# Regrouped early routing, marks shared between two engines, a contiguous overflow list and smaller expert capacities in an attention-plus-experts kernel

## Chip, cores and metric

The kernel runs on one core of a Trainium2 chip. The metric is the device time of one execution in microseconds (us). Three runs of the kernel before gave 647.88, 653.0 and 653.28 us; their median is 653.0 us. One further execution was profiled.

The engines are named as in the profile: PE multiplies matrices (PEld is its weight load), DVE is the vector engine, ACT the scalar engine, POOL the general-purpose engine, SP the engine from which most DMAs are issued. An engine executes its own instructions in order.

## What is computed

Linear attention without a softmax, a normalization of each head, and then a mixture of eight experts in which each token goes to the one expert with the largest logit.

```
kv = einsum('bhsd,bhse->bhde', k, v)            # 8 batches, 8 heads, 576 tokens, 64 columns
out = einsum('bhsd,bhde->bhse', q, kv)
x = out / sqrt(mean(out*out, -1) + 1e-6) * g_norm   # x: 4608 tokens x 512
logits = x @ w_gate;  e_idx = argmax(logits)
gate_w = softmax(logits)[e_idx];  eom = sigmoid(x @ w_output_gate)
for e in range(8):
    mask = e_idx == e
    y[mask] = gate_w[mask] * eom[mask, e] * (relu(x[mask] @ w1[e]) @ w2[e])   # 512 -> 1024 -> 512
```

## The kernel before

**Tiles.** The 4608 tokens are 36 tiles of 128 rows. Attention of a batch is `kv_part` (L413, the product of k and v in five pieces), `kvT_part` (L443, two transposes) and `m_part` (L452); `out_tile` (L482) then makes one tile of 128 tokens, and ACT copies it, squares it and copies its gate products (L512 to L515). The squares are summed by DVE (L528). Tiles are routed in groups: `GR = (8, 8, 10, 10)`. `route` (L532) is a generator of small DVE steps for one group: the norm, the logits, the choice of the expert as a one-hot `ohb` (L607), then on PE a count of earlier tokens of the same expert `rps` (L635 to L644), the token's slot `slots`, and for each tile a mark `la` (L686), a 128x128 matrix that is 1 where the slot's place within its tile is the column. PE multiplies the marks with the slot's tile number, `tblps` (L714), into a table of which token stands in which place; the table gives the row numbers `gidx` for gathers and `oidx` for the scatter of results. `advance` (L748) takes every group that is being routed one step further, up to its next `yield 1`. `PLACES` (L66) says which engine makes the marks of a group: P is POOL, V is DVE.

**Runs.** The experts run in 16 runs (`RUNS`, L54). The first eight take 256 rows of each expert out of the first 16 token tiles (`EARLY = 16`); the last eight take the rest of each expert, in order of how many rows it has, so many rows as `CAP` (L38) leaves for that rank: 704, 704, 640, 620, 600, 576, 576, 576 less 256. Rows beyond the capacity would go through a loop after the last run (L1045), one tile of 128 rows at a time, that loads the expert's weights anew. `mm1` (L272) is the first product of a run, 8 times 12 matmuls whose moving side has as many columns as the run has rows; `mm2` (L295) is the second, for each tile of 128 rows 24 matmuls of 512 columns. Where a run ends in a tile of exactly 64 rows, `half` (L268) is 64 and that tile takes 16 matmuls (L311): the high and the low part of the first product stand side by side. Weights are loaded raw (`wload`, L183, one DMA of 512 KB from SP) and each is split into a high and a low part (`split`, L192, ACT and DVE).

**Order.** Order is written by hand inside the `manual_schedule` blocks. `early` (L769) does the first four batches (`FIRST_B`), tiles 0 to 15, and the routing of the groups 0 and 1; during `while routing` (L803) PE gets eight matmuls on a constant (`constant`, L408, `COLD[2]`) for each round of `advance`. Then come the loads of the second weights of run 0 and the first gather. `late` (L811) is the generator of all other attention and routing; `run` (L971) takes one piece of it after each of its 8 `mm1` steps and one within each `mm2` of the first runs. Loads of the early part go to 22 buffers (`free`), those of the late part to 8 (`xfree`), all issued by SP in order; the writes of x to memory, `xs`, are on SP too. The gathers (`gather`, L228) and the scatters of results (L328) are indirect DMAs from POOL, and POOL also scales gathered rows (`scale_rows`, L243).

**The overflow list.** While runs 7 and 8 go, `overflow_list` (L905) makes a list of the tiles beyond the capacities: `met`, 128 partitions by 44 entries by 2 values. SP writes one of the two values of each entry to memory:

```
959    met = sm.tile([P, NOVER, 2], F32, name="met")
969    nc.sync.dma_start(out=tab, in_=met[:, :, 0])
```

Of the kernel before, what the change touches and what calls it, by code (L numbers as in the profile page):

```python
# [11 lines left out]
F32 = mybir.dt.float32  # L12
# [22 lines left out]
C_SCALE = DM + H  # L35


CAP = [704, 704, 640, 620, 600, 576, 576, 576]  # L38


EARLY = 16
TA = 2
ROWS_A = TA * P
CMAX = max(CAP) - ROWS_A
TMAX = 6

NOVER = NT + E

GR = (8, 8, 10, 10)
GROUPS = [list(range(sum(GR[:i]), sum(GR[:i+1]))) for i in range(len(GR))]  # L50
GMAX = max(GR)
EARLY_GROUP = [sum(GR[:i + 1]) for i in range(len(GR))].index(EARLY)
# [10 lines left out]

APART = (1, 2, 3)

PLACES = ['P', 'PV', 'P', 'P']  # L66

COLD = (2, 20, 8)

ROUND = 1.5 * 2.0 ** 30  # L70

# [51 lines left out]
def body(ctx: ExitStack, tc: tile.TileContext, kvm, rem, qT, wg, gn, w1, w2, kc, xs, tab, out):  # L123
# [143 lines left out]

    def half(i):  # L268

        return P // 2 if RUNS[i][2] % P == P // 2 else 0  # L270

    def mm1(i, f):  # L272

        C = RUNS[i][2]
        T = half(i)
        hi, lo = ([a[:, d] for d in range(4)] for a in xT[i])
        wh, wl = wgt[(1, f // 2)]
        if f == 0:
            w = i // E
            hT[i] = rp_[w].tile([P, 8, 2 * (ROWS_A, CMAX)[w]], F32R, name="hT", tag="hT")  # L280
        ps = ps_h.tile([P, 512], F32, name="hps", tag="h")
        for d in range(4):
            o = d * 256 + (f % 2) * P
            for w, x, k in ((wh, hi, 0), (wh, lo, 1), (wl, hi, 2)):
                nc.tensor.matmul(ps[:, :C], w[:, o:o + P], x[d][:, :C],  # L285
                                 start=(d == 0 and k == 0), stop=(d == 3 and k == 2))
        h = hT[i][:, f]
        nc.scalar.activation(h[:, 0:C], ps[:, :C], AF.Relu)  # L288
        for a, b, l in [(0, C - T, C + T)] + ([(C - T, C, C)] if T else []):
# [5 lines left out]
    def mm2(i, k, events):  # L295
        nonlocal ny
        t, c0, M = tiles_of(i)[k]
        C = RUNS[i][2]
        T = half(i)
        ps = ps_y[0].tile([P, DM], F32, name="yps", tag=f"y{ny % 2}")  # L300
        tl = tails.pop((i, t))
        for f in range(8):
            h = hT[i][:, f]
            wh, wl = wgt[(2, f // 2)]
            w0 = (f % 2) * DM
            w = [a[:, w0:w0 + DM] for a in (wh, wl)]
            if M == T:

                for b in (1, 0) if f == 0 else (0, 1):
                    rows = M + b * M  # L310
                    nc.tensor.matmul(ps[:rows], h[:, c0:c0 + rows], w[1 - b],  # L311
                                     start=(f == 0 and b == 1), stop=(f == 7 and b == 1))
            else:
                hh, hl = h[:, c0:c0 + M], h[:, C + T + c0:C + T + c0 + M]
                for n, (a, b) in enumerate(((hh, w[0]), (hh, w[1]), (hl, w[0]))):
                    nc.tensor.matmul(ps[:M], a, b, start=(f == 0 and n == 0), stop=(f == 7 and n == 2))  # L316
            for e in events.get(f, ()):
                e()
        y = mem.tile([P, DM], F32, name="y", tag=f"y{ny % 3}")
        ny += 1  # L320
        if M == T:
            y2 = mem.tile([P, DM], F32, name="y2", tag="yb")
            nc.scalar.copy(y2[:M], ps[M:2 * M])
# [50 lines left out]
    nq = 0  # L374
    for b in range(B):
        loads += [(kvt, (b, c), kvm[b][:, c]) for c in range(4)]
        if b == 0:
            loads.append((rt, 0, rem[0][0:P // 2]))
        elif b % 2 == 0:
            loads.append((rt, b // 2, rem[b // 2]))  # L380
        if b == 1:
            loads.append((rt, 0, rem[0][P // 2:]))

        bq = b - 1 if b == 0 else b
        while bq >= 0 and nq < -(-tiles_ready(bq) * P // QC):
            loads.append((qt, nq, qT[nq]))
            nq += 1
        if b == B - 1:
            while nq < NTOK // QC:
                loads.append((qt, nq, qT[nq]))  # L390
                nq += 1

    late_loads = [l for l in loads if (l[1] >= EARLY // 2 if l[0] is qt else 2 * l[1] >= FIRST_B if l[0] is rt else l[1][0] >= FIRST_B)]
    loads = [l for l in loads if not any(l is x for x in late_loads)]

    def load(loads, free, spare=0):

        while loads and len(free) > spare:
            where, k, src = loads.pop(0)
            n = src.shape[0]  # L400
            if k in where:
                nc.sync.dma_start(out=where[k][P - n:], in_=src)
                continue
            t = take([P] + list(src.shape[1:]), F32, "ld", free)
            nc.sync.dma_start(out=t[:n], in_=src)
            where[k] = t

    def constant(ps, n, start):  # L408
# [4 lines left out]
    def kv_part(b):  # L413
# [3 lines left out]
        for s in range(5):  # L417
# [17 lines left out]
                give(kvt.pop((b, s)))  # L435
            elif b % 2:
                give(rt.pop(b // 2))
        nc.scalar.copy(augs[b % 3][:, :, 0:D], ps[:, 0:NP * D].rearrange("q (p d) -> q p d", p=NP))
        cp = wk.tile([P, NP * D], F32, name="kvc", bufs=1)
        nc.vector.tensor_copy(cp, ps[:, 0:NP * D])  # L440
        yield cp

    def kvT_part(cp):  # L443
# [88 lines left out]
    def route(gi):  # L532
# [176 lines left out]
        vec.tensor_tensor(out=xtail[:, g0:g0 + n, C_SCALE - DM], in0=se[:, :n], in1=eo[:, :n], op=ALU.mult)  # L709
        xwrite(g0, xs[1 + g0 * P:1 + (g0 + n) * P, DM:XW].rearrange("(t p) x -> p t x", p=P), xtail[:, g0:g0 + n])  # L710
        yield from pause(8)
        tps = ps_t.tile([P, 2, E * TMAX], F32, name="tblps", tag="t")
        for t in range(n):
            nc.tensor.matmul(tps, las[t], rc[:, t, 0:2], start=(t == 0), stop=(t == n - 1))  # L714
# [54 lines left out]
    def early():  # L769

        def more():
            load(loads, free)
            if not loads and not opened[0]:
                open_rows()
            while not loads and w1s and free:
                wload(0, 1, w1s.pop(0))

        w1s = list(range(4))

        more()  # L780
        for b in range(FIRST_B):
            lim = min(tiles_ready(b - 1) if b else 0, EARLY)
            kv = kv_part(b)
            next(kv)
            more()
            run_out(lim)
            next(kv)
            cp = next(kv)
            more()
            run_out(lim)  # L790
            kvT = kvT_part(cp)
            run_out(lim)
            run_out(lim)
            m_part(b, kvT)
            more()
            while run_out(lim):
                more()
        while run_out(EARLY):
            more()
        while squares:  # L800
            sums()
        load(late_loads, xfree, 2)
        while routing:  # L803
            advance()
# [100 lines left out]
    def overflow_list():  # L905
# [63 lines left out]
        nc.sync.dma_start(out=tab, in_=met[:, :, 0])

    def run(i, unit):  # L971

# [170 lines left out]
```

## Time and profile before

| what | us |
|---|---|
| median of three runs | 653.0 |
| the profiled execution, its own time | 652.84 |
| its span, first to last instruction | 651.0 |
| attention, tiles 0 to 15 and routing of groups 0 and 1 | 0 to 83.0 |
| first gather to first expert matmul | 83.0 to 96.2 |
| runs 0 to 6, with the late attention between them | 96.2 to 317.1 |
| run 7 | 317.1 to 346.5 |
| run 8 | 346.5 to 404.9 |
| run 9, of the same size as run 8 | 404.9 to 445.8 |
| runs 10 to 15, to the last matmul | 445.8 to 637.9 |

The span is the profiled execution from its first to its last instruction; 1.84 us of its time lie around it. A row of the timeline gives the start, the duration (or the time to the end of the last, where several are merged), the engine, the line, and in brackets how long the engine had been idle and what ended that. A row of the windows gives a stretch of the span, the busy time of PE, PEld, DVE, ACT and POOL in it with their instructions, the clock that PE was granted as a share of full speed, the share of the 16 DMA engines and the GB/s.

### The profile page before, as it was taken

How to read it: one execution, taken by the hardware profiler on the slowest of the kernel's cores; microseconds unless marked ns; L12 is line 12 of the kernel's file. 1: busy time of each engine (PE TensorE's matmuls, PEld its weight loads, DVE VectorE, ACT ScalarE, POOL GpSimd, SP SyncE). 2: the span in 40 equal slices, each digit the busy share in tenths (PEclk: the TensorE clock that was granted, in tenths of full speed). 3: DMA queues.
4: the chain of work that ended last, by engine and by line, in shares of the span. 5: the costliest groups of instructions: out<-in, count | busy, mean ns of one | idle time of the engine just before them, and what ended most of it. 6: DMA issues, size and time to landing. Idle time of an engine off the chain costs nothing.

```text
span 651.0 us, 12185 instructions
## 1 busy us (share of the span) xinstructions
PE 575.8 (88%) x4825; PEld 498.1 (77%) x4825; DVE 338.1 (52%) x644; ACT 285.7 (44%) x481; POOL 169.6 (26%) x163
## 2 busy tenths in 40 slices
PE   6776829999998988899989759999999999999991
PEld 5664619888887876789878647989899888988881
DVE  1128525645476888575685314544626363647430
ACT  1355015565656844256454213443536353535420
POOL 1001330030303271703613013315050505151101
PEclk9678768999999999899989978999999999999996
DMA  8996465779895573665929977426364645464200
GB/s 287 376 401 243 144 257 180 296 264 360 311 327 205 195 256 120 182 208 179 292 86 122 19 114 252 172 97 210 116 204 143 204 142 190 153 204 135 70 17 17
DMA packets 48395, 126.21 MB, mean 194 GB/s; under 512 B 15490, under 2 KB 15618, under 8 KB 48336
## 3 DMA queue, kind: packets, MB, share of 16 engines
q1 hardware_dynamic: 41440, 105.19, 51.8%
q0 software_dynamic: 6464, 20.00, 10.4%
q8 instruction: 39, 0.64, 0.4%
q10 hardware_dynamic: 432, 0.22, 0.1%
q14 instruction: 20, 0.16, 0.1%
HBM read 106.19 MB, written 19.99 MB: 194 GB/s over the span
## 4 chain that ended last, share of the span: by engine, by line
PE 59%; issue 10%; DMA 8%; DVE 7%; POOL 4%; ACT 2%; POOLq 0%; SPq 0%; DVEq 0%; ACTq 0%
PE yps L316 26%; PE hps L285 24%; DMA wraw<-w 7%; PE tps L261 3%; POOL la L686 2%; DMA xg<-xs,gidx 2%; DVE wlo L218 2%; PE kvps L432 2%; PE ops L507 2%; PE yps L311 1%; ACT whi L215 1%; POOL out L328 1%; PE cps L411 1%; DVE ss L528 1%; DVE gp L577 1%
## 5 line engine op out<-in xcount | busy, mean ns | idle before, releaser
L285 PE MATMUL hps<-xT,whi 128*128 128x256 f32 (+5 forms) x1024 | 228.1, 314 | 10.2 <-DVE hT L290 9.3
L316 PE MATMUL yps<-whi,hT 128*128 128x512 f32 (+2 forms) x592 | 202.8, 406 | 0.0
L285 PEld LDWEIGHTS hps<-xT,whi 128*128 128x128 f32 x1024 | 172.9, 193 | 18.5 <-DVE hT L290 11.0
L285 PE MATMUL hps<-xT,wlo 128*128 128x256 f32 (+5 forms) x512 | 158.6, 310 | 0.0
L316 PEld LDWEIGHTS yps<-whi,hT 128*128 128x128 f32 (+2 forms) x592 | 112.7, 190 | 25.1
L328 POOL DMA_INDIRECT out<-y,oidx x42 | 46.2, 1100 | 299.6 <-ACT y L327 230.2
L290 DVE SCALAR_TENSOR_TENSOR hT<-hps,hT 128x256 fp32r<-128x256 f32 (+4 forms) x168 | 63.9, 400 | 109.3 <-ACT hT L288 102.1
L211 DVE SCALAR_TENSOR_TENSOR wlo<-wraw,gcol,whi 128x1024 fp32r<-128x1024 f32 x64 | 81.8, 1282 | 71.3 <-ACT whi L208 69.2
L316 PE MATMUL yps<-wlo,hT 128*128 128x512 f32 (+2 forms) x296 | 117.6, 397 | 0.0
L288 ACT ACTIVATE hT<-hps 128x256 fp32r<-128x256 f32 (+5 forms) x128 | 55.9, 437 | 140.4 <-PE hps L285 136.1
L285 PEld LDWEIGHTS hps<-xT,wlo 128*128 128x128 f32 x512 | 98.8, 193 | 0.9
L218 DVE TENSOR_TENSOR wlo<-wraw,whi 128x1024 fp32r<-128x1024 f32 x64 | 83.4, 1303 | 23.8 <-ACT whi L215 22.6
L208 ACT ACTIVATE whi<-wraw,gcol 128x1024 fp32r<-128x1024 f32 x64 | 73.3, 1150 | 20.9 <-DMA wraw<-w 20.9
L215 ACT CAST whi<-wraw 128x1024 fp32r<-128x1024 f32 x64 | 66.5, 1040 | 0.0
L241 POOL TENSOR_TENSOR xg<-xg 128x512 f32<-128x512 f32 (+3 forms) x40 | 49.0, 1226 | 67.4 <-DMA xg<-xs,gidx 66.7
L316 PEld LDWEIGHTS yps<-wlo,hT 128*128 128x128 f32 (+2 forms) x296 | 56.5, 191 | 10.5
L264 ACT CAST xT<-tps 128x512 fp32r<-128x512 f32 (+3 forms) x42 | 23.3, 557 | 64.3 <-PE tps L261 63.5
L233 POOL DMA_INDIRECT xg<-xs,gidx x42 | 47.3, 1126 | 15.8 <-issue 14.6
L327 ACT ACTIVATE y<-yps,tl 128x512 f32<-128x512 f32 (+2 forms) x37 | 25.5, 688 | 57.9 <-PE yps L316 42.4
L261 PE MATMUL tps<-ident,xg 128*128 128x128 f32 (+3 forms) x168 | 26.3, 282 | 25.1 <-DVE tl L257 15.9
L261 PEld LDWEIGHTS tps<-ident,xg 128*128 128x128 f32 (+3 forms) x168 | 20.6, 147 | 33.2 <-DVE xg L241 10.0
L686 POOL TENSOR_SCALAR la<-ni,rlon 128x128 bf16<-128x128 f32 x32 | 23.9, 763 | 83.2 <-DVE rlon L659 72.7
(146 smaller groups left out, 438.3 us busy)
## 6 DMA issues: line engine op xcount, KB each, us to landing
wraw<-w SPq DMA_DIRECT2D x128, 512.0 KB, 3.8
ld<-kvm SPq DMA_DIRECT2D x32, 512.0 KB, 7.4
ld<-qT SPq DMA_DIRECT2D x18, 512.0 KB, 5.0
xs<-xrow SPq DMA_DIRECT2D x18, 512.0 KB, 4.3
ld<-rem SPq DMA_DIRECT2D x3, 512.0 KB
xg<-xs,gidx POOLq DMA_INDIRECT x42
out<-y,oidx POOLq DMA_INDIRECT x42
ld<-rem SPq DMA_DIRECT2D x2, 256.0 KB, 10.7
```

What stands on the lines that cost most here:

```text
L208: he.activation(hi, r, AF.Copy, scale=gcol[:, 0:1])
L211: eng.scalar_tensor_tensor(out=lo, in0=r, scalar=gcol[:, 0:1], in1=hi.bitcast(F32), op0=ALU.mult, op1=ALU.subtract)
L215: he.copy(hi, r)
L218: eng.tensor_tensor(out=lo, in0=r, in1=hi.bitcast(F32), op=ALU.subtract)
L233: nc.gpsimd.indirect_dma_start(out=x[:M, :], out_offset=None, in_=rows, in_offset=bass.IndirectOffsetOnAxis(ap=gidx[i // E][:M, p, t:t + 1 ...
L241: eng.tensor_tensor(out=v, in0=v, in1=f, op=ALU.mult)
L261: nc.tensor.transpose(ps[:, c, :M], x[:M, c * P:(c + 1) * P], ident[:M, :M])
L285: nc.tensor.matmul(ps[:, :C], w[:, o:o + P], x[d][:, :C], start=(d == 0 and k == 0), stop=(d == 3 and k == 2))
L288: nc.scalar.activation(h[:, 0:C], ps[:, :C], AF.Relu)
L290: nc.vector.scalar_tensor_tensor(out=h[:, l:l + b - a], in0=ps[:, a:b], scalar=0.0, in1=h[:, a:b].bitcast(F32), op0=ALU.max, op1=ALU.subtract)
L316: nc.tensor.matmul(ps[:M], a, b, start=(f == 0 and n == 0), stop=(f == 7 and n == 2))
L328: i_ = nc.gpsimd.indirect_dma_start(out=out, out_offset=bass.IndirectOffsetOnAxis(ap=oidx[i // E][:M, RUNS[i][0], t:t + 1], axis=0), in_=y ...
```

## The change

The diff has these parts.

1. `CAP` becomes 692, 652, 632, 608, 592, 576, 570, 556, so the last eight runs have 436, 396, 376, 352, 336, 320, 314 and 300 rows, 4878 rows with the first eight in place of 4996. `half` now holds for any last tile of up to 64 rows; the high and low parts stand 64 columns apart, and columns between them are set to zero (two `memset` on DVE a run where they exist). The number of tiles of each run, and which of them are half tiles, stay as they were.
2. Groups of 10, 6, 10, 10 tiles; marks by POOL and DVE in turn in groups 0, 2 and 3, and by DVE, DVE, POOL in group 1; two more pauses ahead of `tblps` in groups 2 and 3.
3. Constants come four at a time, on a buffer of another pool, also three times a batch and once after the fourth in `early`; in `while routing`, seven rounds also take a piece of `late`: the k-v product of batch 4 in three pieces, tiles 16 and 17, the transposes and `m_part` of batch 4. The four loads of k and v of batch 4 are moved ahead of the first weights, into the 22 buffers.
4. The remainder rows of batches 0 and 1 come in one load in place of two halves. In `kv_part` DVE's copy for the transposes stands ahead of ACT's copy.
5. The second weights of run 0 are loaded behind the first gather, with a wait on a POOL instruction that stands after it.
6. `met` becomes two tiles, so that what SP writes is contiguous in each partition.
7. `early` and the runs 0 to 6 stand in one `manual_schedule` block.

```
-CAP = [704, 704, 640, 620, 600, 576, 576, 576]
+CAP = [692, 652, 632, 608, 592, 576, 570, 556]
-GR = (8, 8, 10, 10)
+GR = (10, 6, 10, 10)
-PLACES = ['P', 'PV', 'P', 'P']
-COLD = (2, 20, 8)
+PLACES = ['PV', 'VVP', 'PV', 'PV']
+COLD = (2, 20, 4)
+PIECES = 7
...
-        return P // 2 if RUNS[i][2] % P == P // 2 else 0
+        n = RUNS[i][2] % P
+        return n if n <= P // 2 else 0
...
+        C0 = C - T
+        if T % (P // 2) and f == 0:
+            for c in (C0, C0 + P // 2):
+                nc.vector.memset(hT[i].bitcast(F32)[:, :, c + T:c + P // 2], 0.0)
...
+    late_loads.sort(key=lambda l: l[0] is not kvt or l[1][0] > FIRST_B)
+    loads += late_loads[:4]
+    late_loads = late_loads[4:]
...
-        nc.scalar.copy(augs[b % 3][:, :, 0:D], ps[:, 0:NP * D].rearrange("q (p d) -> q p d", p=NP))
         cp = wk.tile([P, NP * D], F32, name="kvc", bufs=1)
         nc.vector.tensor_copy(cp, ps[:, 0:NP * D])
+        nc.scalar.copy(augs[b % 3][:, :, 0:D], ps[:, 0:NP * D].rearrange("q (p d) -> q p d", p=NP))
...
         yield from pause(8)
+        if g0 >= EARLY:
+            yield 1
+            yield 1
         tps = ps_t.tile([P, 2, E * TMAX], F32, name="tblps", tag="t")
...
+            constants(1)
             kvT = kvT_part(cp)
+            constants(1)
             run_out(lim)
             run_out(lim)
+            constants(1)
             m_part(b, kvT)
...
         while routing:
             advance()
             if routing:
-                constant(ps_t.tile([P, 512], F32, name="cps", tag="t"), COLD[2], True)
+                constants(1)
+                if n < PIECES:
+                    next(rest)
+                    n += 1
+        gather(0)
+        mark = c1.tile([P, 1], F32, name="mark")
+        behind = nc.gpsimd.memset(mark, 0.0)
         for c in range(4):
-            wload(0, 2, c)
-        gather(0)
+            d = wload(0, 2, c)
+            tc.add_manual_dep(d.ins, behind.ins.name, ...)
+
+    def constants(n):
+        constant(ps_h.tile([P, 512], F32, name="cps", tag="h"), n * COLD[2], True)
...
-        met = sm.tile([P, NOVER, 2], F32, name="met")
+        met = [sm.tile([P, NOVER], F32, name=f"met{i}") for i in range(2)]
...
-        nc.sync.dma_start(out=tab, in_=met[:, :, 0])
+        nc.sync.dma_start(out=tab, in_=met[0])
```

More of the change, by code (lines that the diff above doesn't have):

```diff
@@ L43 @@
 ROWS_A = TA * P
-CMAX = max(CAP) - ROWS_A
+CMAX = -(-(max(CAP) - ROWS_A) // (P // 2)) * (P // 2)
 TMAX = 6
 NOVER = NT + E
-GR = (8, 8, 10, 10)
+GR = (10, 6, 10, 10)
 GROUPS = [list(range(sum(GR[:i]), sum(GR[:i+1]))) for i in range(len(GR))]
@@ L287, in mm1 @@
         h = hT[i][:, f]
+        C0 = C - T
+        if T % (P // 2) and f == 0:
+            for c in (C0, C0 + P // 2):
+                nc.vector.memset(hT[i].bitcast(F32)[:, :, c + T:c + P // 2], 0.0)
         nc.scalar.activation(h[:, 0:C], ps[:, :C], AF.Relu)
-        for a, b, l in [(0, C - T, C + T)] + ([(C - T, C, C)] if T else []):
+        for a, b, l in [(0, C0, C0 + P if T else C)] + ([(C0, C, C0 + P // 2)] if T else []):
             nc.vector.scalar_tensor_tensor(out=h[:, l:l + b - a], in0=ps[:, a:b], scalar=0.0,
@@ L309, in mm2 @@
                 for b in (1, 0) if f == 0 else (0, 1):
-                    rows = M + b * M
+                    rows = (1 + b) * P // 2
                     nc.tensor.matmul(ps[:rows], h[:, c0:c0 + rows], w[1 - b],
@@ L313, in mm2 @@
             else:
-                hh, hl = h[:, c0:c0 + M], h[:, C + T + c0:C + T + c0 + M]
+                l0 = C - T + P if T else C
+                hh, hl = h[:, c0:c0 + M], h[:, l0 + c0:l0 + c0 + M]
                 for n, (a, b) in enumerate(((hh, w[0]), (hh, w[1]), (hl, w[0]))):
@@ L322, in mm2 @@
             y2 = mem.tile([P, DM], F32, name="y2", tag="yb")
-            nc.scalar.copy(y2[:M], ps[M:2 * M])
+            nc.scalar.copy(y2[:M], ps[P // 2:P // 2 + M])
             nc.vector.tensor_tensor(out=y[:M], in0=ps[:M], in1=y2[:M], op=ALU.add)
@@ L376, in body @@
         loads += [(kvt, (b, c), kvm[b][:, c]) for c in range(4)]
-        if b == 0:
-            loads.append((rt, 0, rem[0][0:P // 2]))
-        elif b % 2 == 0:
+        if b % 2 == 0:
             loads.append((rt, b // 2, rem[b // 2]))
-        if b == 1:
-            loads.append((rt, 0, rem[0][P // 2:]))
         bq = b - 1 if b == 0 else b
@@ L399, in load @@
             where, k, src = loads.pop(0)
[L400 to L403, printed above, removed]
             t = take([P] + list(src.shape[1:]), F32, "ld", free)
-            nc.sync.dma_start(out=t[:n], in_=src)
+            nc.sync.dma_start(out=t, in_=src)
             where[k] = t
@@ L802, in early @@
         load(late_loads, xfree, 2)
+        n = 0
         while routing:
@@ L805, in early @@
             if routing:
-                constant(ps_t.tile([P, 512], F32, name="cps", tag="t"), COLD[2], True)
-        for c in range(4):
-            wload(0, 2, c)
-        gather(0)
+                constants(1)
+                if n < PIECES:
[4 more added lines that the diff above has]
+        behind = nc.gpsimd.memset(mark, 0.0)
+        for c in range(4):
+            d = wload(0, 2, c)
+            tc.add_manual_dep(d.ins, behind.ins.name,
+                              mybir.DependencyInfo(mybir.DependencyClass.Sync, mybir.DependencyReason.DATA),
+                              reason="order of the transfers")
+    def constants(n):
+        constant(ps_h.tile([P, 512], F32, name="cps", tag="h"), n * COLD[2], True)
     def late():
@@ L958, in overflow_list @@
         yield
-        met = sm.tile([P, NOVER, 2], F32, name="met")
+        met = [sm.tile([P, NOVER], F32, name=f"met{i}") for i in range(2)]
         vec.tensor_tensor(out=sel2, in0=sel, in1=c0.unsqueeze(1).to_broadcast(shp), op=ALU.mult)
-        vec.tensor_reduce(out=met[:, :, 0], in_=sel2, axis=AX.X, op=ALU.add)
+        vec.tensor_reduce(out=met[0], in_=sel2, axis=AX.X, op=ALU.add)
         yield
-        vec.tensor_tensor(out=met[:, :, 0], in0=met[:, :, 0], in1=iv, op=ALU.add)
-        vec.tensor_scalar(out=met[:, :, 0], in0=met[:, :, 0], scalar1=float(P), scalar2=None, op0=ALU.mult)
+        vec.tensor_tensor(out=met[0], in0=met[0], in1=iv, op=ALU.add)
+        vec.tensor_scalar(out=met[0], in0=met[0], scalar1=float(P), scalar2=None, op0=ALU.mult)
         vec.tensor_tensor(out=sel2, in0=sel, in1=cf[:, K_E:K_E + E].unsqueeze(1).to_broadcast(shp), op=ALU.mult)
         yield
-        vec.tensor_reduce(out=met[:, :, 1], in_=sel2, axis=AX.X, op=ALU.add)
-        vec.tensor_copy(meti, met[:, :, 1])
-        nc.sync.dma_start(out=tab, in_=met[:, :, 0])
+        vec.tensor_reduce(out=met[1], in_=sel2, axis=AX.X, op=ALU.add)
+        vec.tensor_copy(meti, met[1])
+        nc.sync.dma_start(out=tab, in_=met[0])
     def run(i, unit):
@@ L1013, in run @@
             drop(2, c)
+    rest = late()
     with tc.manual_schedule(engines=MAN):
@@ L1019, in body @@
             ps_p.clear()
-    rest = late()
-    ps_y[0] = main.enter_context(tc.tile_pool(name="ps_y", bufs=1, space=psum))
-    with tc.manual_schedule(engines=MAN):
+        ps_y[0] = main.enter_context(tc.tile_pool(name="ps_y", bufs=1, space=psum))
         split(0, 1, 0)
```

## The prediction, made before the result was known

> **What bounds the kernel now.** I read the page first (busy shares and slices), then windows cut at the stages, then the timeline where a window's PE is not full, then the chain for the price of one step.
>
> ```profile
> PE 575.8 (88%) x4825; PEld 498.1 (77%) x4825; DVE 338.1 (52%) x644; ACT 285.7 (44%) x481; POOL 169.6 (26%) x163
> PEclk9678768999999999899989978999999999999996
> GB/s 287 376 401 243 144 257 180 296 264 360 311 327 205 195 256 120 182 208 179 292 86 122 19 114 252 172 97 210 116 204 143 204 142 190 153 204 135 70 17 17
> ```
>
> PE is the bound at 88%, so what counts is where it is not busy or not at full clock. The slices, 16.3 us each, show two such places: the first six, with a clock of 6 to 8 tenths, and the 22nd to 25th, where the DMA falls to 19 GB/s and the clock then to 7.
>
> ```profile
> 61.50:83.00 21.50, 14.09 (x97) 10.50 (x95) 13.23 (x62) 0.47 (x2) 8.92 (x13) 0.76 0.55 171
> 83.00:96.20 13.20, 2.20 (x9) 1.43 (x9) 2.75 (x6) 1.23 (x3) 6.41 (x6) 0.57 0.75 297
> 96.20:131.00 34.80, 34.62 (x406) 30.03 (x407) 20.13 (x26) 20.10 (x34) 1.03 (x1) 0.92 0.66 230
> 232.40:269.00 36.60, 29.16 (x204) 24.84 (x203) 27.93 (x60) 14.88 (x24) 17.35 (x19) 1.00 0.60 188
> 346.50:404.90 58.40, 47.18 (x204) 39.41 (x203) 18.63 (x35) 16.96 (x25) 11.04 (x11) 0.88 0.94 113
> 404.90:445.80 40.90, 40.90 (x197) 35.27 (x196) 19.45 (x32) 16.67 (x23) 11.49 (x11) 1.00 0.43 142
> ```
>
> From 61.5 to 83.0 PE's work is mostly constants, and to 96.2 it waits for the gather. Run 0 (third row) leaves PE no gap. In 232.4 to 269.0 PE lacks 7.4 us. Runs 8 and 9 (last two rows) have the same 448 rows; run 8 takes 58.40 us and run 9 40.90.
>
> **The overflow list (part 6).**
>
> ```profile
> 344.52 0.66 SPq L969 DMA_DIRECT2D tab<-met  x1
> ...
> 387.79 1.15 ACT L208 ACTIVATE whi<-wraw,gcol 128x1024 fp32r<-128x1024 f32 x1 [19.96 <-DMA wraw<-w]
> ...
> DMA packets 7633, 7.10 MB, mean 118 GB/s; under 512 B 5920, under 2 KB 5920, under 8 KB 7630
> tab<-met SPq DMA_DIRECT2D x1, 22.0 KB
> ```
>
> SP sends 22 KB at 344.52. One value of each pair is taken, so it goes as 128 x 44 = 5632 pieces of 4 bytes, and the packets of 340 to 400 us (third row) hold 5920 under 512 B. The weights queued behind it reach ACT only at 387.79, after ACT sat idle for 19.96 us. A contiguous list is one piece of 176 B in each partition, 128 in all, a 44th of the count. By the two windows the jam costs 58.40 - 40.90 = 17.5 us; PE's idle time in run 8 alone is 58.40 - 47.18 = 11.2, the rest is the lower clock (0.88) and the bunching of waits. I take 17.5, since run 9 has the same matmuls, and keep 11.2 as the low end. Late next: nothing within some 40 us, as run 9 shows.
>
> **The capacities (part 1).**
>
> ```profile
> 404.85 19.46 PE hps L285 x96
> ...
> 547.77 14.08 PE hps L285 x96
> ```
>
> 448 rows take 19.46 us for the first product, 320 rows 14.08: 0.0420 us a row. The list falls by 118 rows, so 118 x 0.0420 = 5.0 us. The second product keeps its matmuls, as tiles and half tiles stay. The new zeroing on DVE waits for what `hT`'s first write waits for anyway and lies under the 12 matmuls of the first step: nothing; uncovered, eight of them at some 0.3 us (estimate from the marks' 0.326 below) would be 2.4.
>
> **The seven pieces (part 3).**
>
> ```profile
> 99.64 1.91 PE kvps L432 x32
> ...
> 103.34 0.71 PE ops L507 x32
> ...
> 105.67 1.08 PE kvps L432 x32
> ...
> 108.38 0.71 PE ops L507 x32
> ...
> 110.72 0.61 PE kvps L432 x16
> ```
>
> These are, in the chain of run 0, the pieces that move into the wait for routing. PE was full there, so 1.91 + 0.71 + 1.08 + 0.71 + 0.61 = 5.0 us leave the path (transposes and the small product left out). In their new place PE had constants. Their loads: batch 4's k and v move ahead of the first weights, on a queue that moves 287 to 401 GB/s through the first three slices; what then comes later (weights, writes of x) is needed after 80 us. The load for tiles 16 and 17 goes out after tile 15, as before. SP is moved past nothing that the routing needs, but PE is (a rival below).
>
> **Marks and pauses in group 3 (part 2).**
>
> ```profile
> 260.92 7.39 POOL L686 TENSOR_SCALAR la<-ni,rlon 128x128 bf16<-128x128 f32 x10 [2.09 <-DVE rhk L660]
> ...
> 263.53 0.30 PE L714 MATMUL tblps<-rrc,la 128*128 128x96 bf16 x3
> ...
> 268.37 0.22 PE L714 MATMUL tblps<-rrc,la 128*128 128x96 bf16 x1 [0.36 <-POOL la L686]
> ```
>
> POOL makes ten marks in 7.39 us, and PE stands behind them from 263.53 to 268.59, 5.1 us, where ten matmuls at 0.1 need 1.0. With five marks on POOL (3.7 us) and two pieces more before `tblps`, the 4.1 us go. For that DVE gets ten marks more in groups 2 and 3, at 0.326 us each (row below) 3.3 us; DVE is idle for 36.60 - 27.93 = 8.7 us in that window, yet in order, so some delay evictions that PE waits for. I charge 1.0, with 0 and 3.3 as ends. Net 3.1.
>
> **The early routing and the first gather (parts 2, 3, 5).**
>
> ```profile
> 68.50:75.20 6.70, 6.64 (x34) 5.14 (x33) 3.61 (x14) 0.47 (x2) 0.00 (x0) 0.55 0.40 130
> ...
> 70.57 0.23 DVE L607 TENSOR_TENSOR ohb<-rsc,rsx 128x64 bf16<-128x64 f32 x1
> ...
> 75.19 0.21 PE L635 MATMUL rps<-erow,row 128*128 128x72 bf16 x1
> ...
> 76.69 2.96 POOL L686 TENSOR_SCALAR la<-ni,rlon 128x128 bf16<-128x128 f32 x4 [8.38 <-PE cps L411]
> ...
> L686 DVE TENSOR_SCALAR la<-ni,rlon x4: 274/326/379, 77.0 to 78.9; 128x128 bf16<-128x128 f32 x4
> ...
> 79.38 0.17 DVE L709 TENSOR_TENSOR xtail<-rdn 128x8 f32<-128x8 f32 x1
> 80.05 1.96 SPq L188 DMA_DIRECT2D wraw<-w  x4
> ...
> 82.97 1.09 POOL L233 DMA_INDIRECT xg<-xs,gidx  x1 [3.32 <-issue]
> ...
> 89.91 0.69 DVE L241 TENSOR_TENSOR xg<-xg 128x512 f32<-128x512 f32 x1 [8.94 <-DMA xg<-xs,gidx]
> ...
> 269.83 1.00 POOL L233 DMA_INDIRECT xg<-xs,gidx  x1 [0.30 <-issue]
> ...
> 273.33 1.05 POOL L241 TENSOR_TENSOR xg<-xg 128x512 f32<-128x512 f32 x1 [1.24 <-DMA xg<-xs,gidx]
> ```
>
> The first gather starts at 82.97 and its rows are used at 89.91, 6.9 us later; four weight loads had been issued at 80.05, just ahead of it. A gather with little beside it, at 269.83, needed 3.5 us to 273.33. The second weights now wait until it has been issued, so I take 6.9 - 3.5 = 3.4 us; ends 0 (the loads follow at once and share the DMA engines) and 3.4. They then land some 4 us later, and run 0 needs them only after its first steps.
>
> The gather cannot start before the last `xtail` (79.38) is in memory. Up to there DVE bounds the routing, with two waits on PE; in one of them `ohb` is ready at 70.80 and `rps` starts at 75.19, 4.4 us behind constants. Afterwards: DVE's 13.2 us in the first window grow by 2.9 (group 0 has ten tiles and two rounds more left after tile 15, five of its marks are DVE's), plus 0.4 for batch 4's copy, less 0.8 for six tiles in place of eight: 15.7. PE between tile 15 and the second `rps` has constants, two k-v pieces, two tiles and two small products, 12 us at the low clock by the rows above doubled, so `rps` is about 1.3 late, and two groups in step save about 1.5 by overlap. 61.5 + 15.7 + 1.3 - 1.5 = 77.0, an estimate, against 79.55: 2.5 us. Ends 0 (the pieces hold the routing as the constants did) and 6 (it becomes as short as DVE's old 13.2).
>
> A page speaks against marks on both engines at once: the Trainium skill, GPSIMD Engine Reference, section 1 (SBUF interfaces), says that POOL shares its interfaces with VectorE, with contention against DVE instructions that have two SBUF inputs or run in a 2-port mode. Taken as no overlap at all, group 1's two POOL and four DVE marks would cost about 1.3 us more, and the sum would be 617.6. The trace does not show it for marks: four beside a working DVE took 2.96, ten took 7.39, 0.74 each both times. Without these sentences the sum stands as it is.
>
> The rest of parts 3, 4 and 7 I cost at nothing: constants stand where PE waits for copies (cover gone: 13 calls of four at 0.21, the low-clock price in the 6.70 us window, 11 us of PE, most of it in the first 50 us, which the loads pace); the whole remainder load brings 256 KB ahead of batch 1 and takes them away behind it; one copy ahead of the other saves at most 0.4 a batch.
>
> **Sum.** 651.0 - 17.5 - 5.0 - 5.0 - 3.1 - 3.4 - 2.5 = 614.5 us span, and with the 1.84 us around it (652.84 - 651.0) 616.3. The profiled execution stands 0.2 below the median of 653.0, so 616 holds for both.
>
> **Rivals.** (a) The pieces hold the routing. PE is in order, and a late q for tile 16 would stop everything behind it, `rps` and `tblps` too. For it: constants did just that (70.80 to 75.19). Against: the DMA share there is 0.55. Then the 2.5 are lost and as much again: 621. (b) The jam is not the list's, but that of whatever run 8 loads, or the contiguous list is still slow: 616.3 + 17.5 = 634. Against it: run 9's loads are of the same kind and stall nothing. (c) The other side: the smaller capacities overflow. The loop after the last run then makes each extra tile alone: 36 marks at 0.326 (11.7), a gather (6.9), 4 MB of weights at about 400 GB/s (10.5), its matmuls and the rest (about 9): 38 us, an estimate. One tile gives 654, no change; from two tiles on it is slower, 692. The reference's routing of its default inputs, padded to 256 early rows, gives by rank 660, 646, 620, 607, 584, 557, 556, 502 rows: all fit, one by a single row, so it is unlikely. (d) Run 8 gets back only its idle 11.2 us: 622.6, within the range.
>
> **Numbers.** My forecast, 0.78: 616, with (d) in it. (a) 0.13: 621. (b) 0.05: 634. (c) 0.04: 654 or 692, half each. The range leaves out (b) and (c) and little more: low 606 (routing 6 in place of 2.5, no charge on DVE, PE's remaining gaps in 232 to 269 closing by 4 more, and a warmer start), high 630 (early gain 0, list 11.2, DVE's charge 3.3). Faster by over 1% (about what a measurement of this kernel tells from no change) 0.96, within 1% 0.02, slower 0.02.
>
> **What would show it.** In the changed kernel's trace: run 8 about as long per row as run 9, no idle ACT before its weights; `tblps` of group 3 without gaps; no attention of batch 4 after the first expert matmul; that matmul near 90 us, the first rows used some 3.5 us after the first gather; the runs 8 to 15 shorter by 0.042 us a row. Wrong would be: run 8 still over 50 us, a first expert matmul after 95 us, new DVE waits in runs 4 to 6, or any instruction of the overflow loop.

## The result, and the profile after

The changed kernel takes 614.03 us (median of four runs, 613.19 to 614.87), the kernel before 651.46 (four runs beside them, 647.88 to 653.28). The ratio is 0.943, with a 95% interval of 0.938 to 0.948. The forecast was 616.0. The profiled execution took 614.2 us, its span 612.4.

First the page of the changed kernel: busy time of PE, then PE's clock and the DMA rate in 40 slices of 15.3 us.

```profile
PE 556.8 (91%) x4829; PEld 484.0 (79%) x4829; DVE 338.2 (55%) x666; ACT 285.7 (47%) x481; POOL 156.8 (26%) x149
PEclk9989859999999988999999999999999999999996
GB/s 310 406 405 329 328 235 220 371 256 311 234 244 200 246 155 161 241 210 202 276 157 238 129 103 209 121 162 165 151 185 125 218 145 207 141 217 137 42 19 17
```

Both weak places have shrunk. Ahead of the last slice the clock falls below 8 in one, the sixth (the first gather), and no slice ahead of the last three moves less than 103 GB/s, where one of before moved 19. PE's busy time fell by 19.0 us (575.8 to 556.8), the span by 38.6: about half the gain is idle time.

The windows of the changed kernel at the stages that the prediction showed (columns as there):

```profile
61.50:79.40 17.90, 11.86 (x193) 8.88 (x190) 14.64 (x68) 5.12 (x14) 4.82 (x7) 0.79 0.84 278
79.40:89.40 10.00, 2.79 (x9) 1.72 (x9) 2.80 (x6) 1.94 (x3) 4.61 (x6) 0.50 0.76 257
89.40:123.60 34.20, 34.19 (x411) 29.84 (x412) 21.25 (x28) 20.42 (x37) 3.36 (x3) 0.94 0.86 303
224.20:253.80 29.60, 26.69 (x181) 24.13 (x180) 22.44 (x53) 14.05 (x23) 10.51 (x11) 0.94 0.55 171
329.50:370.50 41.00, 41.00 (x202) 35.54 (x201) 18.55 (x34) 16.88 (x24) 11.38 (x11) 1.00 0.47 157
370.50:409.20 38.70, 38.70 (x197) 34.50 (x196) 19.04 (x34) 16.30 (x23) 11.36 (x11) 1.00 0.47 152
```

Run 8 (fifth row) has no idle PE and full clock; its 41.00 us for 436 rows and run 9's 38.70 for 396 are 0.094 and 0.098 us a row. Taking the first matmul of each run from the timeline, the span divides like this:

| stage | before | after | difference | predicted |
|---|---|---|---|---|
| to the first expert matmul | 96.2 | 88.7 | -7.5 | -5.9 |
| runs 0 to 3 | 136.1 | 135.4 | -0.7 | with the next row |
| runs 4 and 5 | 60.9 | 53.5 | -7.3 | -8.1 for both rows |
| run 6 | 23.8 | 23.8 | 0.0 | 0 |
| run 7 | 29.7 | 27.9 | -1.8 | 0 |
| run 8 | 58.0 | 41.0 | -17.0 | -18.0 |
| runs 9 to 15, to the last matmul | 233.2 | 229.0 | -4.2 | -4.5 |
| behind the last matmul | 13.1 | 13.1 | 0.0 | 0 |

The timeline of the changed kernel around the first gather and around the last group's marks:

```profile
64.89 0.78 PE L513 MATMUL ops<-aug,ld 64*64 64x80 f32 x32 [2.15 <-DMA ld<-qT]
...
76.34 0.17 DVE L715 TENSOR_TENSOR xtail<-rdn 128x6 f32<-128x6 f32 x1
...
79.42 1.09 POOL L236 DMA_INDIRECT xg<-xs,gidx  x1 [3.94 <-DVE wlo L214]
...
83.01 0.69 DVE L244 TENSOR_TENSOR xg<-xg 128x512 f32<-128x512 f32 x1 [4.20 <-DMA xg<-xs,gidx]
...
88.68 1.30 PE L289 MATMUL hps<-xT,whi 128*128 128x256 f32 x2 [0.68 <-ACT xT L267]
...
231.41 3.48 POOL L692 TENSOR_SCALAR la<-ni,rlon 128x128 bf16<-128x128 f32 x5 [2.59 <-DVE rlon L665]
231.43 0.50 DVE L692 TENSOR_SCALAR la<-ni,rlon 128x128 bf16<-128x128 f32 x2
...
233.46 0.70 DVE L692 TENSOR_SCALAR la<-ni,rlon 128x128 bf16<-128x128 f32 x3
234.60 0.41 DVE L299 SCALAR_TENSOR_TENSOR hT<-hps,hT 128x256 fp32r<-128x256 f32 x1
235.06 0.50 PE L289 MATMUL hps<-xT,whi 128*128 128x256 f32 x2 [2.91 <-DVE hT L299]
236.62 1.02 PE L724 MATMUL tblps<-rrc,la 128*128 128x96 bf16 x10
```

The gather starts at 79.42 (82.97 before) and its rows are used 3.6 us later (6.9 before). The late q of tile 16, the mechanism of rival (a), holds PE for 2.15 us. The ten `tblps` now go without a gap in 1.02 us, but the five marks on DVE stand in front of an `hT`, and PE waits 2.91 us for it: the charge that the prediction put at 1.0.

The chain of waits shows the price of a row as before:

```profile
329.46 18.99 PE hps L289 x96
370.47 17.28 PE hps L289 x96
...
510.00 14.07 PE hps L289 x96
```

(18.99 - 14.07) / (436 - 320) = 0.0424 us a row.

### The profile page after: what moved, and what is told of

Read it like the earlier page. It is cut to its first block, busy times and chain, and to the rows that moved or that the text cites. A ratio compares the mean times of both kernels' runs of the same rounds, so it can differ in the third digit from the quotient of the medians.

```text
span 612.4 us, 12185 instructions
## 1 busy us (share of the span) xinstructions
PE 556.8 (91%) x4829; PEld 484.0 (79%) x4829; DVE 338.2 (55%) x666; ACT 285.7 (47%) x481; POOL 156.8 (26%) x149
## 4 chain that ended last, share of the span: by engine, by line
PE 70%; issue 11%; DVE 6%; DMA 6%; ACT 3%; POOL 2%; another core or an unknown queue 1%; ACTq 0%; POOLq 0%; SPq 0%; DVEq 0%
PE yps L326 30%; PE hps L289 27%; PE ops L513 4%; PE tps L264 3%; PE kvps L438 3%; DMA ld<-qT 2%; DVE wlo L221 2%; DMA xg<-xs,gidx 1%; PE yps L320 1%; DMA wgs<-wg 1%; POOL out L338 1%; PE cps L417 1%; ACT whi L218 1%; DVE hT L299 1%; DMA xs<-xrow 1%
## 5 line engine op out<-in xcount | busy, mean ns | idle before, releaser
L289 PE MATMUL hps<-xT,whi 128*128 128x256 f32 (+8 forms) x1024 | 222.4, 309 | 10.1 <-DVE hT L299 8.8
L326 PE MATMUL yps<-whi,hT 128*128 128x512 f32 (+3 forms) x592 | 200.3, 402 | 0.0
L289 PE MATMUL hps<-xT,wlo 128*128 128x256 f32 (+8 forms) x512 | 156.2, 305 | 0.0
L326 PEld LDWEIGHTS yps<-whi,hT 128*128 128x128 f32 (+3 forms) x592 | 110.8, 187 | 24.7
L299 DVE SCALAR_TENSOR_TENSOR hT<-hps,hT 128x256 fp32r<-128x256 f32 (+9 forms) x168 | 62.9, 395 | 102.8 <-ACT hT L297 94.9
L326 PE MATMUL yps<-wlo,hT 128*128 128x512 f32 (+3 forms) x296 | 116.5, 394 | 0.0
L297 ACT ACTIVATE hT<-hps 128x256 fp32r<-128x256 f32 (+8 forms) x128 | 55.4, 433 | 118.7 <-PE hps L289 113.5
L326 PEld LDWEIGHTS yps<-wlo,hT 128*128 128x128 f32 (+3 forms) x296 | 55.6, 188 | 10.7
L244 POOL TENSOR_TENSOR xg<-xg 128x512 f32<-128x512 f32 (+8 forms) x40 | 49.4, 1240 | 33.8 <-DMA xg<-xs,gidx 32.8
L513 PE MATMUL ops<-aug,ld 64*64 64x80 f32 x1152 | 29.5, 238 | 11.1 <-DMA ld<-qT 5.1
```

Source lines behind the costliest of these rows:

```text
L244: eng.tensor_tensor(out=v, in0=v, in1=f, op=ALU.mult)
L289: nc.tensor.matmul(ps[:, :C], w[:, o:o + P], x[d][:, :C], start=(d == 0 and k == 0), stop=(d == 3 and k == 2))
L513: nc.tensor.matmul(ps[c0:c0 + D, u, p * W:(p + 1) * W], qt[g // 2][r, p, q0:q0 + D], augs[b % 3][r, p, :], start=True, stop=True)
```

## The experiments

Runs e1 to e4, e5 to e8 and e9 to e12 were each timed beside the kernel before (medians 651.24, 651.83 and 649.6). Each undoes or changes one part of the changed kernel (e10 builds on e8, e12 on e11), except e9, which starts from the kernel before. "Cost" is the median less 614.03. The intervals of the ratios are about 0.007 wide to each side, so costs of 1 or 2 us are read from the traces, not from the medians.

There is one trace of each, and the stages vary between traces too. In the changed kernel and in e1, e2, e5 and e6, which all have its early part, the last `xtail` comes between 75.7 and 77.5 us and the first expert matmul between 87.9 and 89.8. From that matmul to run 6 the changed kernel and the runs that keep its pieces and marks (e1, e2, e4, e7, e8, e10, e11) take 187.0 to 190.1 us. A difference that stays inside these ranges shows nothing.

**e1: the list in pairs again.**

```
-        met = [sm.tile([P, NOVER], F32, name=f"met{i}") for i in range(2)]
+        mt = sm.tile([P, NOVER, 2], F32, name="met")
+        met = [mt[:, :, i] for i in range(2)]
```

> The changed kernel with the overflow list in pairs again, so that SP sends 5632 pieces of 4 bytes. My theory (the list alone made the jam): the time rises by 17.5 us, from 614.0 to about 631.5, run 8 takes about 58 us in place of 41.0, ACT is idle for about 20 us ahead of a weight of run 9. Rival 1 (only PE's idle time was the list's): about 625. Rival 2 (the jam was another load's, and is gone with the new order): 614 and run 8 stays at 41.

630.05 us, ratio 0.967 (0.960 to 0.974): cost 16.0. The windows of runs 8 and 9 in e1, then its ACT and its packets from 322 to 385 us:

```profile
329.70:385.20 55.50, 44.06 (x202) 37.58 (x201) 18.32 (x35) 16.70 (x24) 11.77 (x11) 0.88 1.05 116
385.20:423.90 38.70, 38.70 (x197) 34.51 (x196) 19.06 (x34) 16.31 (x23) 10.83 (x11) 1.00 0.45 150
```

```profile
370.36 1.15 ACT L211 ACTIVATE whi<-wraw,gcol 128x1024 fp32r<-128x1024 f32 x1 [19.97 <-DMA wraw<-w]
```

```profile
GB/s 0 0 190 317 264 268 45 11 17 38 55 52 27 20 19 7 18 26 6 2 33 24 48 30 40 36 50 39 55 31 336 414 398 421 414 385 161 271 0 239
DMA packets 7775, 7.57 MB, mean 120 GB/s; under 512 B 5940, under 2 KB 5940, under 8 KB 7772
```

The whole picture of before is back: run 8 at 55.5 us, ACT idle for 19.97 before its weights, the clock at 0.88, and 24 of these 1.6 us slices (some 38 us) at 55 GB/s or less. In the changed kernel the same stretch has 606 packets under 512 B.

```profile
DMA packets 3161, 10.56 MB, mean 168 GB/s; under 512 B 606, under 2 KB 606, under 8 KB 3156
```

The 5334 packets of difference are about the 5632 - 128 = 5504 that the layouts differ by. Run 9 is the same in both. Rivals (b) and (d) fall: 14.5 us of run 8 come back, not 0 and not 11.2.

**e9: the list alone, in the kernel before.**

```
-        met = sm.tile([P, NOVER, 2], F32, name="met")
+        mt = [sm.tile([P, NOVER], F32, name=f"mt{i}") for i in range(2)]
...
-        nc.sync.dma_start(out=tab, in_=met[:, :, 0])
+        nc.sync.dma_start(out=tab, in_=mt[0])
```

> The kernel before the change with nothing but the contiguous overflow list. My theory (the list alone made the jam; 16.0 us were its price in the changed kernel, 17.5 by the windows before): the time falls from 651.5 by 16 to 17.5 us, to 634 to 635.5, run 8 takes 41 to 42 us in place of 58, and ACT's wait of 19.96 us for a weight is gone. Rival (the old order has something else that holds run 8): less than 12 us.

635.81 us, ratio 0.978 (0.970 to 0.986), 13.8 below the median beside it. The windows of runs 8 and 9 in e9:

```profile
342.90:384.40 41.50, 41.50 (x201) 35.53 (x200) 18.72 (x34) 17.12 (x24) 10.86 (x11) 1.00 0.46 156
384.40:425.40 41.00, 41.00 (x198) 35.32 (x198) 18.73 (x32) 16.66 (x23) 11.70 (x11) 1.00 0.43 144
```

Run 8 falls from 58.0 to 41.5, by 16.5, and stands half a microsecond above its twin. So the list is worth 14.5 (e1) to 16.5 us (e9) of run 8, more than the 11.2 and less than the 17.5; e1 lies about halfway between the two. Run 7 falls too, from 29.7 to 28.0, as in the changed kernel, a gain of 1.8 that the prediction did not have. That the list brings it is not shown: in e1 run 7 takes 28.0 with the pairs, and in e4 29.9 without them.

**e2: the old capacities.**

```
-CAP = [692, 652, 632, 608, 592, 576, 570, 556]
+CAP = [704, 704, 640, 620, 600, 576, 576, 576]
```

> The changed kernel with the old capacities, 118 rows more. My theory (each row costs 96 matmul columns, 0.0420 us, and nothing else): 614.0 + 5.0 = 619.0; runs 8 and 9 grow by 0.5 and 2.2 us. Rival (the sizes that are no multiple of 64 cost something of their own, and zeroing on DVE stalls PE): the time rises by 2.5 us or less.

619.8 us, ratio 0.951 (0.944 to 0.958): cost 5.8. Runs 8 and 9 take 41.5 and 40.9 us; from the first matmul of run 8 to that of run 15 it is 245.6 us against 241.6, 4.0 more for 98 rows (0.041 a row). The other nine runs with the new capacities and the contiguous list take 241.9 to 242.9 there, so by them it is 2.7 to 3.7. The rest lies ahead of run 8 (start 331.4 against 329.3), where nothing in the edit acts: the spread of the early stages.

**e3: no pieces in the wait for routing.**

```
-PIECES = 7
+PIECES = 0
```

> The changed kernel without the seven pieces in the wait for routing; only four constants stand in each round. My theory (the pieces leave the path of the runs, whichever run then has fewer of them, and hold the routing by 1 to 2 us because tile 16 waits for its q): the first expert matmul comes 1 to 2 us earlier than 88.7, the runs 0 to 4 take 5.0 us more than their 164.4 together, the time is 614.0 + 5.0 - 1.5 = 617.5. Rival 1 (the pieces were free where they were, in gaps of the runs): 612.5. Rival 2 (the pieces cost the routing nothing): 619.

618.77 us, ratio 0.952 (0.944 to 0.958): cost 4.7 by the medians, 2.1 by the profiled spans (614.5 and 612.4). The timeline of e3:

```profile
74.23 0.17 DVE L715 TENSOR_TENSOR xtail<-rdn 128x6 f32<-128x6 f32 x1
...
77.42 1.10 POOL L236 DMA_INDIRECT xg<-xs,gidx  x1 [4.05 <-DVE wlo L214]
...
86.69 1.30 PE L289 MATMUL hps<-xT,whi 128*128 128x256 f32 x2 [0.68 <-ACT xT L267]
```

Without the pieces the routing ends 2.1 us earlier (74.23 against 76.34), and the first matmul comes 2.0 earlier. From there to run 6 it takes 192.5 us against 188.9. So by this pair the pieces bring 3.6 and cost 2.0. Both lie outside the ranges given above, so their signs are shown; by the ends of these ranges the gain is 2.4 to 5.5 and the cost 1.2 to 3.1. That the pieces hold the routing, rival (a), is there, and loses.

**e4: second weights ahead of the gather, with no wait.**

```
+        for c in range(4):
+            wload(0, 2, c)
         gather(0)
-        mark = c1.tile([P, 1], F32, name="mark")
-        behind = nc.gpsimd.memset(mark, 0.0)
-        for c in range(4):
-            d = wload(0, 2, c)
-            tc.add_manual_dep(d.ins, behind.ins.name, ...)
```

> The changed kernel with the second weights of run 0 issued ahead of the first gather again, without the wait. My theory: the first rows are used about 6.9 us after the gather starts in place of 3.6, the first expert matmul comes 3.3 us later, and nothing gives that back: 617.3. Rival (the weights then come sooner and run 0 runs better, or the gather was slow for another reason): within 1 us of 614.0.

619.55 us, ratio 0.951 (0.945 to 0.958): cost 5.5. The timeline of e4:

```profile
76.38 1.97 SPq L191 DMA_DIRECT2D wraw<-w  x4
...
78.86 1.09 POOL L236 DMA_INDIRECT xg<-xs,gidx  x1 [3.95 <-DVE wlo L214]
...
86.03 0.69 DVE L244 TENSOR_TENSOR xg<-xg 128x512 f32<-128x512 f32 x1 [7.88 <-DMA xg<-xs,gidx]
...
91.69 1.30 PE L289 MATMUL hps<-xT,whi 128*128 128x256 f32 x2 [0.68 <-ACT xT L267]
```

The gather starts a little earlier (78.86), but its rows are used 7.2 us later in place of 3.6: 2 MB on the queues in front of it cost 3.6 us, and the first matmul comes 3.0 later. Runs 5 to 7 add 3.8 (25.2, 24.6, 29.9 us against 24.2, 23.8, 27.9), and runs 0 to 4 give 1.7 back (163.0 against 164.7); why runs 5 to 7 lengthen was not followed up. A part is the spread of the stages: run 5 takes 25.2 in e1 too, and run 6 24.6 in e5, e6 and e11.

**e5: the old marks.** **e6: the pauses kept, marks on POOL alone.**

```
-PLACES = ['PV', 'VVP', 'PV', 'PV']
+PLACES = ['PV', 'VVP', 'P', 'P']
...
-        if g0 >= EARLY:
-            yield 1
-            yield 1
```

(e6 has the first of these two edits only.)

> The changed kernel with the marks of groups 2 and 3 on POOL alone and without the two extra pauses, as before the change. My theory: PE stands about 4 us behind POOL's marks in group 3, DVE's stalls of PE in runs 3 and 4 (now 4.95 us) fall by about 1, the time rises by 3.1 us to 617. Rival (DVE's new marks took back what POOL's gave): within 1 us of 614.0.

> The changed kernel with the marks of groups 2 and 3 on POOL alone, but with the two extra pauses. It tells the pauses from the engines. If the pauses do it all (ten marks at 0.74 us lie under three pieces): 613 to 615, no gap between the tblps matmuls. If DVE's help is needed too: 616 to 617, PE still 2 us or more behind the marks.

e5: 620.18 us, ratio 0.952 (0.945 to 0.958), cost 6.2. e6: 620.98 us, ratio 0.953 (0.946 to 0.961), cost 7.0. What PE waited for around the two late groups, in e5 (186 to 262 us; total, times, longest):

```profile
PE tblps L720 <- POOL la L692: 6.6, 13, 1.2
PE tblps L720 <- DVE rrc L709: 2.7, 1, 2.7
PE hps L289 <- DVE hT L299: 1.3, 1, 1.3
```

in e6 (186 to 260):

```profile
PE hps L289 <- DVE hT L299: 3.2, 2, 1.9
PE tps L264 <- issue: 3.0, 1, 3.0
PE tblps L724 <- POOL la L692: 2.5, 5, 1.2
```

and in the changed kernel (190 to 253):

```profile
PE hps L289 <- DVE hT L299: 5.0, 3, 2.9
PE tps L264 <- issue: 2.2, 1, 2.2
```

In the kernel before (198 to 269 us) the same view has

```profile
PE hps L285 <- DVE hT L290: 4.3, 4, 1.7
PE tblps L714 <- POOL la L686: 3.2, 7, 1.1
```

In the changed kernel no `tblps` waits. In e5 PE stands for POOL's marks 13 times, in both groups (3.2 us in group 2, 3.4 in group 3), where the kernel before stood for one group only: with the other changes in place, group 2 would stand as well. So undoing costs more than the 3.1 of the prediction: 6.2 by the medians, of which 5.3 lie between the first expert matmul and run 6 (194.2 us against 188.9). The pauses alone (e6) cut POOL's part to 2.5 us and do not bring the time back: that stretch takes 192.3 us, still above the 187.0 to 190.1 of the runs with shared marks. The change of place does. It is not free: waits for `hT` grow from 1.3 to 5.0.

**e7: groups of eight again, with the new marks for the late groups.**

```
-GR = (10, 6, 10, 10)
+GR = (8, 8, 10, 10)
-PLACES = ['PV', 'VVP', 'PV', 'PV']
+PLACES = ['P', 'PV', 'PV', 'PV']
```

> The changed kernel with early groups of eight and eight, the first marked by POOL alone and the second by POOL and DVE in turn, as before the change. My theory: the routing to the last xtail takes about 2.5 us longer (78.8 in place of 76.3), the first expert matmul comes at about 91.2, the time is 616.5. Rival (the grouping gives nothing, all of the early gain is that of the constants and of the gather): the first expert matmul within 0.7 us of 88.7, the time 614.

614.95 us, ratio 0.945 (0.938 to 0.952): no difference to be measured. The timeline of e7:

```profile
77.39 0.17 DVE L715 TENSOR_TENSOR xtail<-rdn 128x8 f32<-128x8 f32 x1
...
89.85 1.31 PE L289 MATMUL hps<-xT,whi 128*128 128x256 f32 x2 [0.68 <-ACT xT L267]
```

The routing ends 1.05 us later than in the changed kernel and the first matmul comes 1.2 later, but both times lie inside the ranges that the runs with ten and six show (77.39 in 75.7 to 77.5; e1, with ten and six, has its first matmul at 89.83). So this trace shows no worth of the grouping.

**e8: no constants in the first four batches.** **e10: the same, with eight constants a round in place of four.**

```
-            constants(1)
             kvT = kvT_part(cp)
-            constants(1)
             run_out(lim)
             run_out(lim)
-            constants(1)
             m_part(b, kvT)
...
-        constants(1)
```

```
-COLD = (2, 20, 4)
+COLD = (2, 20, 8)
```

> The changed kernel without the constants that stand within the four early batches and behind them; those of the routing stay. My theory (they cost and give nothing, loads and ACT set the pace there): the clock granted in the first 53 us falls from 0.97 to about 0.8, the last square of tile 15 comes within 1 us of where it is, the time is 613 to 615. Rival (the warm clock is what holds that stretch where it is): the first expert matmul 2 us or more later than 88.7, 616 or more.

> The kernel of the run before last without early constants, and with eight constants in each round of the routing in place of four. If the constants are what held the old routing on PE: the last xtail comes 1.5 us or more later than 75.75 and the time rises from 613.8 to 615.5 or more. If DVE and the load for tile 16 set the pace and PE has room: xtail within 0.7 us of 75.75, the time within 1 us of 613.8.

e8: 613.77 us, ratio 0.942 (0.935 to 0.948). e10: 614.7 us, ratio 0.945 (0.937 to 0.953). Neither differs measurably from the changed kernel. In e8 the last `xtail` comes at 75.75 and the first matmul at 88.35, 0.3 ahead of the changed kernel; in e10 at 76.86 and 89.14. By this pair eight constants a round cost the routing 1.1 us over four, which is inside the range that equal early parts show. The early ones buy nothing: without them the last square of tile 15 is done at 57.6 (e8) and 58.2 (e10), in the changed kernel at 59.9, against the expectation that it would move by less than 1 us.

**e11: q of tiles 16 and 17 loaded early, with batch 4's k and v.** **e12: the same, and a pause within the last group's step.**

```
-    late_loads.sort(key=lambda l: l[0] is not kvt or l[1][0] > FIRST_B)
-    loads += late_loads[:4]
-    late_loads = late_loads[4:]
+    first = [l for l in late_loads if l[0] is qt and l[1] == EARLY // 2 or l[0] is kvt and l[1][0] == FIRST_B]
+    late_loads = [l for l in late_loads if not any(l is x for x in first)]
+    loads += first
```

```
-        if not last:
-            yield from pause(7)
+        yield from pause(7)
```

> The changed kernel with the q of tiles 16 and 17 loaded ahead of the first weights, with batch 4's k and v. My theory: PE's wait of 2.15 us for that load is gone, the routing is shorter by 1.5 to 2 us, the first expert matmul comes at about 87, the time is 612.3. Rival (DVE sets the pace anyway, the wait on the load was beside it): the first expert matmul within 0.5 us of 88.7, 614.0.

> As the run before, and the last group's routing pauses between its two halves of marks as the other groups' does. My theory: DVE's block of 4.3 us in one piece, behind which PE stood 2.91 us at 235, is cut in two, PE's stall falls to about 1 us, and the time is 2 us below that of the run before, 610.3. Rival (the stall only moves to the next piece): no difference from the run before by more than 0.7 us.

e11: 614.36 us, ratio 0.944 (0.939 to 0.950), no gain. Its timeline:

```profile
73.22 0.42 DVE L445 COPY kvc<-kvps 128x256 f32<-128x256 f32 x1 [2.93 <-PE kvps L438]
...
77.00 0.17 DVE L715 TENSOR_TENSOR xtail<-rdn 128x6 f32<-128x6 f32 x1
...
89.22 1.30 PE L289 MATMUL hps<-xT,whi 128*128 128x256 f32 x2 [0.68 <-ACT xT L267]
```

The routing ends 0.7 later than in the changed kernel, not earlier. Yet DVE did not set the pace alone, and the 2.15 us of q did not lie beside its work. In the changed kernel DVE stands 1.33 us for `rex`, which ACT makes only behind its copies of tile 16, and these wait for q:

```profile
67.25 0.24 DVE L704 TENSOR_REDUCE rdn<-rex 128x10 f32<-128x80 f32 x1 [1.33 <-ACT rex L653]
```

In e11 that wait is gone, and this step comes at 65.23. Then DVE stands 2.93 us for PE's last k-v product of batch 4, where the changed kernel has 0.43: from 68.3 to 77.0 PE is granted a clock of 0.50 (0.89 in the changed kernel), and four constants take 1.06 us in place of 0.62. What q gave is lost at PE. Why the clock is lower there is not shown.

e12 was meant to break up the 2.91 us stall before 235.06; it takes 617.85 us, ratio 0.950 (0.944 to 0.956), and the stall is longer:

```profile
236.99 0.51 PE L289 MATMUL hps<-xT,whi 128*128 128x256 f32 x2 [4.00 <-DVE hT L299]
```

No version tried here beats the changed kernel measurably.

## Why the prediction was right, step by step

- **The list (17.5).** Shown from both sides: 16.0 by e1, 13.8 by e9, 14.5 and 16.5 of run 8 in their traces. Taking run 9 as the measure of run 8 without the jam was sound; PE's idle time alone (11.2) would have been too little. The term was 1 to 4 us too large; 0.4 of that comes from where the windows begin and end, since by their first matmuls runs 8 and 9 differ by 17.1.
- **The capacities (5.0).** Shown: 2.7 to 4.0 us for the 98 rows between the first matmuls of runs 8 and 15, where the prediction's price makes 4.1, and 0.042 us a row of first product in the chain. No instruction of the overflow loop's body runs, so rival (c) did not come about.
- **The pieces (5.0).** Shown in its sign, too large in its size: by e3 3.6 gained after the first matmul, 2.0 lost ahead of it. 2.3 of the 3.6 lie in runs 0 to 3 (137.7 us against 135.4) and 1.4 in runs 4 and 5. Against the kernel before, runs 0 to 3 shorten by 0.7 only and runs 4 and 5 by 7.3. The late routing has moved up as well (the `tblps` of group 2 begin at 207.6 in place of 236.6 us, in run 3 and no longer in run 4; those of group 3 at 236.6 in place of 263.5, in run 4 and no longer in run 5); how much each part adds to the 7.3 is not separated.
- **Marks and pauses (3.1).** Too small for the changed kernel, whose group 2 would stand too (6.2 by e5, 5.3 of it up to run 6). Together these two steps were put at 8.1, and the runs 0 to 6 gave 8.0 (0.7 + 7.3). That they agree so well is partly luck, since one was too large and the other too small.
- **The charge on DVE (1.0).** PE stood for `hT` for 4.3 us in the kernel before and stands for 5.0 now, 0.7 more, but much else differs between the two. Against e5, which differs in marks and pauses alone, it is 3.7 (1.3 to 5.0), above the upper end of 3.3 that the prediction gave; the net gain was larger all the same, because two groups no longer stand.
- **The second weights (3.4).** Shown: 3.6 between gather and first use, 3.0 at the first matmul (e4).
- **The early routing (2.5).** The last `xtail` moved from 79.38 to 76.34, 3.0 us; by all traces, from 78.5 and 79.4 (e9 and before, with the old early part) to 75.7 to 77.5, 1.1 to 3.7. The 2.5 lie inside, but the working behind them is not borne out: the regrouping was to save by six tiles in place of eight and by overlap, and e7 shows no worth of it; DVE was to bound it but for two waits on PE, and it waits 1.33 us for ACT in the changed kernel and 2.93 for PE in e11. What is gone is the wait of `rps` behind constants: 4.4 us before, 0.5 in the changed kernel (70.47 to 70.95). Eight constants a round do not bring it back (0.9 in e10), so which of the changes removed it is not separated.
- **Costed at nothing.** Shown for the early constants (e8). The others were not tried.
- **The total.** 616.0 against 614.03 is closer than its terms: the list was too large by 1 to 4 us, marks and pauses too small by 2 to 3, and run 7's 1.8 stood in no term. That the errors nearly cancel is luck.
- **Contention of marks.** The marks of the late groups in e5, then in the changed kernel (columns: least, median and largest duration in ns, first and last start):

```profile
L692 POOL TENSOR_SCALAR la<-ni,rlon x20: 590/599/1450, 197.7 to 238.3; 128x128 bf16<-128x128 f32 x20
```

```profile
L692 DVE TENSOR_SCALAR la<-ni,rlon x10: 272/276/310, 198.4 to 233.8; 128x128 bf16<-128x128 f32 x10
L692 POOL TENSOR_SCALAR la<-ni,rlon x10: 595/712/982, 198.4 to 234.3; 128x128 bf16<-128x128 f32 x10
```

The medians on POOL (599 and 712 ns) mix different neighbours. In group 3, ten marks without DVE's help take 7.29 us in e5 and five with it 3.48 us in the changed kernel, 0.73 and 0.70 each, so the means show no slowing of POOL by marks on DVE, and the marks on DVE stay at 276. Single marks beside them take 0.64 to 0.82 us in the late groups, so a small one is not excluded. What slows them more is other work of DVE: in e5 a mark takes 0.60 us where DVE is idle (the last five of group 3), and the two that run beside `wlo<-wraw,whi` (from 234.08) take 1.9 together in place of 1.2. The prediction's 0.74 for ten marks was such a mixture: one of them took 1.47 us beside `wlo`, the last six 0.60. The Trainium skill, GPSIMD Engine Reference, section 1 (SBUF interfaces), says that the two engines share these interfaces, with contention where a VectorE instruction has two SBUF inputs or runs in a 2-port mode. The trace agrees for `wlo`, which reads two tiles. The sum with no overlap of marks (617.6) did not come about.

## What to carry to other kernels

When two stages do the same work, the time of the undisturbed one is the measure of what the disturbed one can win back; its idle time alone is too low, because the clock suffers as well (0.88 against 1.00 in run 8). Look at the packets under 512 B before looking at the bytes: a list of 22 KB can hold up megabytes of weights behind it. Work that is moved into a wait pays a part of what it saves to whatever ends that wait, and a stall that is removed at one place can come back in part or whole at another (the marks: from POOL to DVE; the late q: from ACT's copies to PE's k-v product), so undo one part at a time and read the stage, not only the total. Compare a stage over several traces of equal code before calling a microsecond a gain.

## What the runs showed of the hardware

A higher granted clock brought nothing where loads set the pace. These are the windows of the first 53 us in the changed kernel,

```profile
0.00:53.00 53.00, 39.25 (x892) 32.06 (x892) 14.23 (x36) 20.52 (x49) 3.20 (x7) 0.97 0.98 377
```

and in e8, without the early constants:

```profile
0.00:53.00 53.00, 40.00 (x872) 33.59 (x876) 15.03 (x36) 21.02 (x52) 3.19 (x7) 0.84 0.98 377
```

The clock is 0.97 against 0.84, the DMA share 0.98 and the rate 377 GB/s in both, and e8 is the earlier of the two at the first matmul (88.35 against 88.68). Over e1, e2, e5, e6, e7 and e10 as well, this clock lies between 0.89 and 1.00 and the rate at 376 or 377. In the routing it was otherwise: in e11 DVE waited for PE, and there four constants took 1.06 us at 0.50 and 0.62 at 0.89. And 5632 pieces of 4 bytes, 22 KB in all, kept the rate at or below 55 GB/s for some 38 us, about 7 ns a piece over 16 DMA engines (38 us / 5632, an estimate), on a chip that moves about 400 GB/s in other slices of the same run.
